# Five gradient stores cut into a 120-partition part from SyncE and an 8-partition part from ScalarE

## The chip, the core and the metric

The kernel runs on one core of a Trainium2 chip. The core has five engines that run beside each other: TensorE (PE in the profile; its weight loads are PEld), VectorE (DVE), ScalarE (ACT), GpSimd (POOL) and SyncE (SP), which here does nothing but issue transfers. Transfers between the chip's memory (HBM) and the on-chip memory of 128 partitions (SBUF) are carried out by 16 DMA engines. The metric is the time of one execution on the device, in microseconds (us).

## What is computed

The reference is the forward pass and all gradients of a decoder block for a single new token in each of B = 4 sequences: layer norm, attention with 32 heads over a cache of 4096 keys and values of size 128, output projection, then layer norm and a gated feed-forward part. What matters here are the gradients of the cache:

```python
q = ((_layernorm(x) @ wq).reshape(B, 1, H, Dh)).transpose(0, 2, 1, 3)
scores = jnp.einsum("bhqd,bhkd->bhqk", q, k_cache) * (Dh ** -0.5)
p = _softmax(scores, axis=-1)
o = jnp.einsum("bhqk,bhkd->bhqd", p, v_cache)
...
_out, _vjp = jax.vjp(_f, A_x, A_k_cache, A_v_cache, A_wq, A_wo, B_w1, B_w3, B_w2)
_grads = _vjp(grad_out)
```

For each of the B x H = 128 heads the gradient of the keys, dK = dS (outer product) q, and that of the values, dV = p (outer product) dO, are each a block of 4096 x 128 numbers in bf16, 1 MB. Reading K once and V twice and writing dK and dV moves about 640 MB.

## The kernel before, in words

A head is a tile of 128 partitions; each partition holds 32 consecutive rows of 128 numbers, which are 8 KB and contiguous in HBM on both sides. Such tiles live in 23 slots (class `Slot`): taking a slot waits until its last user is done, which for a stored tile is the landing of its store.

Two passes run over the heads. The first one loads K and V of each head, computes scores, softmax and the forward output. After a short middle part (feed-forward, its gradient, and the start of the gradient of the attention output) the second pass loads V again and works through the heads in steps of its main loop (L1252), where step s does the following:

- `load_ahead` issues the load of a later head's V on SyncE (L797).
- `front` (L1166) transposes V of head s + 5 on TensorE in groups of eight (L764), copies each group back on ScalarE (L765), and multiplies with dO (L1182). Every fourth head, ScalarE copies the result (L1157), TensorE transposes it (L1164), and `group_dS` turns it into dS for four heads on VectorE (L1196, L1199).
- `more_V` calls `grad_V` (L777), which makes the dV tile of a head some steps ahead on VectorE (the outer product of L770) and has SyncE store it (L781).
- `grad_K` (L1202) makes the dK tile of head s in the same way, and has SyncE store it (L1206).
- `step` adds a piece of the remaining work: the gradients of the weights, which are also stored by SyncE (L1101 is one of these).

The order on every engine is the order of the program, written by hand. Every transfer that SyncE or ScalarE issues gets one of eight completion semaphores in rotation; before it is issued, the transfer that last had the same semaphore must have landed. As SyncE alone issues such transfers in this kernel, it keeps eight of them in flight. At the end of the kernel SyncE waits for all that is outstanding (L1298).

At the end of the second pass V is all loaded and the weights' gradients are out; what is left in SyncE's queue is dV and dK in turn, then, as dV runs ahead, the last four dK stores in a row. The heads are called dK 0 to dK 127 and dV 0 to dV 127 in what follows.

Of the kernel before, what the change touches and what calls it, by code (L numbers as in the profile page):

```python
# [24 lines left out]
def kernel(  # L25
# [22 lines left out]
    nc = tc.nc  # L48
    P = nc.NUM_PARTITIONS
# [7 lines left out]
    NH = B * H  # L57
# [26 lines left out]
    def bh_of(s):  # L84
        return s % B, s // B

    def rows_of(ap):
        return ap.rearrange("(p j) d -> p j d", p=P)
# [89 lines left out]
    def ones_window(col):  # L178
# [11 lines left out]
                          in_=rowg[:, None, :, None].to_broadcast([P, 4, 8, 4]))  # L190
# [578 lines left out]
    def outer(dst, col2, row):  # L769
        nc.vector.tensor_tensor(  # L770
            out=dst.rearrange("p j (r t) -> p j r t", t=2),
            in0=col2[:, :, None, :].to_broadcast([P, SJ, Dh // 2, 2]),
            in1=row.rearrange("p (r t) -> p r t", t=2)[:, None, :, :].to_broadcast([P, SJ, Dh // 2, 2]),
            op=ALU.mult,
        )
# [151 lines left out]
    with ExitStack() as c2:  # L927
# [274 lines left out]
        def grad_K(s):  # L1202
            b, h = bh_of(s)
            gk = Slot("gk")
            outer(gk.heads(), dS2s[s // B][:, s % B], reps["rq", s // REP][:, s % REP, :])
            nc.sync.dma_start(out=rows_of(out_2[b, h]), in_=gk.heads())  # L1206
            gk.give()

        def prefetch():
# [42 lines left out]
        for s in range(NH):  # L1252
            load_ahead(s + L)
            if s % REP == 2:
                replicate("rq", s + 2)
            if s + L < NH:
                front(s + L)
            elif s + L == NH:
                rows_out()
                rows_T()  # L1260
            if s > 0:
                more_V(s + 1 + lead_V(s))
            grad_K(s)
            if s % B == B - 1 and s + 1 < NH:
                group_dS((s + 1) // B)
            if O0 <= s < S0:
                step("o")
            if s >= S1:
                step("s", 2)
            elif s >= O0:  # L1270
                step("q")
# [31 lines left out]
```

## Time and profile before

| | before |
|---|---|
| time, median of 3 runs | 1702.98 us (1702.85 to 1703.41) |
| span of the profiled execution | 1700.1 us |
| busy: PE, DVE, ACT, POOL | 73%, 73%, 57%, 24% |
| moved by DMA | 707.50 MB, mean 416 GB/s |
| dK stores | 128 of 1024 KB, 20.1 us from issue to landing (median) |
| dV stores | 128 of 1024 KB, 20.0 us |
| second loads of V | 128 of 1024 KB, 19.9 us |
| one dK or dV tile on VectorE | 2.29 us |
| first and last of SyncE's last ten issues | 1657.23 and 1679.34 us |

The busy shares of the engines say how long each worked, not what limits. The rows of transfers tell from issue to landing, which holds the time in the queue as well as the time of the transfer itself. The mean rate says how well the 16 DMA engines are used together. Times inside the span are counted from its start.

### The profile page before, as it was taken

The numbers are of one execution on the slowest core, as the hardware profiler recorded it, in microseconds if no ns is written. First come the engines' busy times: TensorE is split into PE (matmuls) and PEld (weight loads), VectorE is DVE, ScalarE is ACT, GpSimd is POOL, SyncE is SP. The second block draws the span as 40 slices with busy tenths as digits, with TensorE's granted clock in tenths as the row PEclk, the third lists the DMA queues.
The fourth block names the chain that finished last, engine by engine and source line by source line (L and its number), as shares of the span: only waits on it lengthen the run. The fifth ranks groups of instructions, "written<-read, shape, count | busy, mean of one in ns | idle before, by whom it ended". The sixth has DMA issues, their size and how long they took to land.

```text
span 1700.1 us, 38407 instructions
## 1 busy us (share of the span) xinstructions
PE 1242.4 (73%) x16180; PEld 915.5 (54%) x16180; DVE 1236.5 (73%) x1294; ACT 968.9 (57%) x1502; POOL 406.4 (24%) x678
## 2 busy tenths in 40 slices
PE   5889888888888888877877664786676566586550
PEld 4777676666666666655655443443444343344330
DVE  5989999999998997667776665674557466566672
ACT  3555444544454444677766564676677566576550
POOL 1211222222222231324352111142112222210120
PEclk8999999999999999799899897977799778777775
DMA  9999999999999999999999999999999999999996
GB/s 401 424 424 424 424 424 424 424 423 424 417 422 412 423 405 400 385 415 425 425 424 426 425 426 426 425 426 426 425 423 420 419 423 417 423 420 414 416 423 275
DMA packets 101741, 707.50 MB, mean 416 GB/s; under 512 B 11052, under 2 KB 15288, under 8 KB 17600
## 3 DMA queue, kind: packets, MB, share of 16 engines
q1 hardware_dynamic: 101152, 704.95, 99.4%
q8 instruction: 127, 2.08, 0.5%
q14 instruction: 46, 0.38, 0.1%
q0 software_dynamic: 416, 0.10, 0.0%
HBM read 422.59 MB, written 282.34 MB: 415 GB/s over the span
## 4 chain that ended last, share of the span: by engine, by line
DMA 37%; ACT 10%; PE 7%; issue 1%; DVE 1%; DVEq 0%; SPq 0%; ACTq 0%; POOL 0%
DMA out_dram<-gv 14%; DMA out_dram<-gk 12%; DMA V<-in_A_v_cache_dram 9%; ACT V L765 9%; PE pt_tps L764 2%; PE dq_ps L962 2%; PE dP_ps L1182 2%; DMA out_dram<-gwo 1%; DVE gk L770 1%; DVE gv L770 1%; PE rep_ps L1133 0%; ACT dPr L1157 0%; PE pt_wo L574 0%; ACT reps L1136 0%; PE o_ps L1059 0%
## 5 line engine op out<-in xcount | busy, mean ns | idle before, releaser
L765 ACT COPY V<-pt_tps 128x1024 bf16<-128x1024 bf16 x512 | 490.2, 1024 | 132.9 <-PE pt_tps L764 128.5
L764 PE MATMUL pt_tps<-ident_b,V 128*128 128x128 bf16 x4096 | 353.3, 247 | 192.4 <-ACT V L765 152.9
L764 PEld LDWEIGHTS <-V 128*128 128x128 bf16 x4096 | 303.1, 113 | 264.0 <-issue 199.0
L770 DVE TENSOR_TENSOR gv<-P,reps 128x4096 bf16<-128x4096 bf16 x125 | 286.3, 2293 | 191.3 <-DMA out_dram<-gv 100.3
L770 DVE TENSOR_TENSOR gk<-dS,reps 128x4096 bf16<-128x4096 bf16 x128 | 293.1, 2292 | 103.8 <-DMA out_dram<-gv 89.8
L421 DVE TENSOR_TENSOR PK<-Kn,PK 128x4096 bf16<-128x4096 bf16 x128 | 292.3, 2284 | 26.1 <-POOL PK L417 25.7
L436 PE MATMUL M_ps<-PK,Vn 128*128 128x130 bf16 x4096 | 284.3, 221 | 32.8 <-DMA Vn<-in_A_v_cache_dram 32.0
L436 PEld LDWEIGHTS <-Vn 128*128 128x128 bf16 x4096 | 252.0, 99 | 53.2 <-DMA Vn<-in_A_v_cache_dram 45.5
L328 DVE STREAM_TRANSPOSE KT<-Kn 128x512 f32<-128x512 f32 (+1 forms) x321 | 250.6, 797 | 0.3 <-issue 0.2
L323 ACT COPY KT<-pt_tps 128x1024 bf16<-128x1024 bf16 x128 | 129.5, 1012 | 186.4 <-PE pt_tps L322 153.0
L1182 PE MATMUL dP_ps<-V,zd 128*32 128x512 bf16 x1024 | 181.2, 431 | 68.0 <-ACT V L765 64.6
L1152 POOL COPY P<-P_all 128x64 bf16<-128x64 bf16 x125 | 100.5, 806 | 447.3 <-DVE gv L770 440.0
L1147 POOL COPY zd<-dOT_bf 128x2 bf16<-128x2 bf16 x128 | 131.4, 1028 | 155.3 <-PE dP_ps L1182 155.2
L334 POOL TENSOR_TENSOR W<-qrep,wmask 128x128 bf16<-128x128 bf16 x128 | 123.8, 967 | 82.4 <-PE S_ps L354 67.6
L417 POOL COPY PK<-P_all 128x64 bf16<-128x64 bf16 x128 | 32.6, 254 | 414.3 <-ACT P_all L411 411.3
L1182 PEld LDWEIGHTS <-zd 128*32 128x32 bf16 x1024 | 37.7, 95 | 156.5 <-issue 141.8
L411 ACT COPY P_all<-pt_P 32x64 bf16<-32x64 bf16 x256 | 52.1, 203 | 53.1 <-PE pt_P L407 50.8
L322 PE MATMUL pt_tps<-ident_b,Kn 128*128 128x128 bf16 x1024 | 80.4, 223 | 0.0
L446 PE MATMUL kP_ps<-PK,onesw 128*32 128x512 bf16 x1024 | 79.1, 386 | 0.0
L386 ACT ACTIVATE E<-S_ps,nm 128x256 f32<-128x256 f32 x64 | 30.4, 474 | 80.4 <-DVE nm L383 80.4
L322 PEld LDWEIGHTS <-Kn 128*128 128x128 bf16 x1024 | 62.0, 100 | 25.8 <-issue 25.8
L354 PE MATMUL S_ps<-KT,W 128*32 128x256 bf16 x1536 | 75.3, 285 | 0.5 <-DVE KT L328 0.2
(239 smaller groups left out, 1226.0 us busy)
## 6 DMA issues: line engine op xcount, KB each, us to landing
Kn<-in_A_k_cache_dram SPq DMA_DIRECT2D x128, 1024.0 KB, 15.4
Vn<-in_A_v_cache_dram SPq DMA_DIRECT2D x128, 1024.0 KB, 15.6
V<-in_A_v_cache_dram SPq DMA_DIRECT2D x128, 1024.0 KB, 19.9
out_dram<-gv SPq DMA_DIRECT2D x128, 1024.0 KB, 20.0
out_dram<-gk SPq DMA_DIRECT2D x128, 1024.0 KB, 20.1
wq<-in_A_wq_dram SPq DMA_DIRECT2D x8, 1024.0 KB, 15.5
out_dram<-gw SPq DMA_DIRECT2D x6, 896.0 KB, 19.8
wo<-in_A_wo_dram SPq DMA_DIRECT2D x4, 1024.0 KB, 11.7
```

The source lines that it names most:

```text
L322: nc.tensor.transpose(pt[:, i, :], Kn[:, c * GW + i, :], ident_b[:])
L323: nc.scalar.copy(out=KT[:, c * GW:(c + 1) * GW, :], in_=pt[:])
L328: nc.vector.transpose(out=KT[:, c * w_:(c + n) * w_], in_=Kn[:, c * w_:(c + n) * w_])
L334: nc.gpsimd.tensor_tensor(out=W[:, hl], in0=qrep[:, :, s:s + 1].to_broadcast([P, 4, 32]), in1=wmask[:, hl, None, :].to_broadcast([P, 4, 32 ...
L421: nc.vector.tensor_tensor(out=PK[:, :, 0:Dh].rearrange("p j (r t) -> p j r t", t=2), in0=Ks[s].heads().rearrange("p j (r t) -> p j r t", t=2),
L436: nc.tensor.matmul(hold["M"][:], lhsT=Vn[:, j, :], rhs=PK[:, j, :], start=(j == 0), stop=(j == SJ - 1))
L764: nc.tensor.transpose(pt[:, i, :], v[:, g * GW + i, :], ident_b[:])
L765: nc.scalar.copy(out=v[:, g * GW:(g + 1) * GW, :], in_=pt[:])
L770: nc.vector.tensor_tensor(out=dst.rearrange("p j (r t) -> p j r t", t=2), in0=col2[:, :, None, :].to_broadcast([P, SJ, Dh // 2, 2]), in1=r ...
L1147: nc.gpsimd.tensor_copy(out=zd[s % B][:, 32:132:67], in_=dOT_bf[:, s:s + 1].to_broadcast([P, 2]))
L1152: nc.gpsimd.tensor_copy(out=P2s[s][:], in_=P_all[:, s, :, None].to_broadcast([P, SJ, 2]))
L1182: nc.tensor.matmul(rows["acc"][32 * c:32 * (c + 1), :], lhsT=zq_window(zd[hl], 2 * hl + u), rhs=VT[:, j0:j0 + 4, :], start=(hl == 0 and u ...
```

## The change

The stores of dK for the last five heads (123 to 127) are cut in two. The first 120 partitions are issued by SyncE as before; the last 8 partitions go out as a transfer of their own, 64 KB, which ScalarE issues. It is meant to change how the rows of these last stores are spread over the DMA engines: a store of 128 rows and one of 120 and one of 8 rows need not be split in the same way.

```diff
-            nc.sync.dma_start(out=rows_of(out_2[b, h]), in_=gk.heads())
+            dk = rows_of(out_2[b, h])
+            if s < NH - 5:
+                nc.sync.dma_start(out=dk, in_=gk.heads())
+            else:
+                nc.sync.dma_start(out=dk[0:P - 8], in_=gk.heads()[0:P - 8])
+                nc.scalar.dma_start(out=dk[P - 8:P], in_=gk.heads()[P - 8:P])
             gk.give()
```

The line numbers of the changed kernel are higher by two for the whole stores (L1208); the parts stand at L1210 (SyncE) and L1211 (ScalarE).

## The prediction

> **What bounds the kernel now.** I read the slices of the page first, then the end of the run in stretches.
>
> ```profile
> DMA  9999999999999999999999999999999999999996
> GB/s 401 424 424 424 424 424 424 424 423 424 417 422 412 423 405 400 385 415 425 425 424 426 425 426 426 425 426 426 425 423 420 419 423 417 423 420 414 416 423 275
> ...
> q1 hardware_dynamic: 101152, 704.95, 99.4%
> ```
>
> The 16 DMA engines are busy throughout at about 424 GB/s; no compute engine is above 73%. Only the last slice (42.5 us) falls, to 275 GB/s. I cut it up (columns: stretch, length, busy us of PE, PEld, DVE, ACT, POOL, then clock, DMA share, GB/s):
>
> ```profile
> 1660.00:1680.00 20.00, 0.00 (x0) 0.00 (x0) 6.31 (x3) 0.00 (x0) 0.00 (x0) 0.50 1.01 426
> 1680.00:1684.00 4.00, 0.00 (x0) 0.00 (x0) 0.00 (x0) 0.00 (x0) 0.00 (x0) 0.50 0.91 385
> 1684.00:1686.00 2.00, 0.00 (x0) 0.00 (x0) 0.00 (x0) 0.00 (x0) 0.00 (x0) 0.50 0.33 139
> 1686.00:1690.00 4.00, 0.00 (x0) 0.00 (x0) 0.00 (x0) 0.00 (x0) 0.00 (x0) 0.50 0.06 27
> 1690.00:1694.00 4.00, 0.00 (x0) 0.00 (x0) 0.00 (x0) 0.00 (x0) 0.00 (x0) 0.50 0.06 27
> 1694.00:1698.00 4.00, 0.00 (x0) 0.00 (x0) 0.00 (x0) 0.00 (x0) 0.00 (x0) 0.50 0.06 27
> ```
>
> From 1686 on the DMA share is 0.06, one sixteenth: **one DMA engine works alone** while fifteen have finished, between about 1683 and 1686. The DMA view of 1686 to 1698 counts what it still moves:
>
> ```profile
> DMA packets 44, 0.32 MB, mean 27 GB/s; under 512 B 5, under 2 KB 5, under 8 KB 5
> ```
>
> 44 packets, of which 5 are semaphore writes: 39 rows of 8 KB in 12 us, so 0.306 us a row, and one transfer (128 rows over 16 engines, 8 rows each) takes an engine 8 x 0.306 + 0.006 = 2.454 us, which is the spacing of SyncE's last issues ((1679.34 - 1654.77)/10 = 2.457). Meanwhile SyncE only waits:
>
> ```profile
> SPq L1298 <- DMA out_dram<-gk: 18.9, 2, 16.6
> ```
>
> The last store is issued at 1679.34 and lands after 19.4 us (the smallest time of the gk transfers) at 1698.8; 1.3 us later the span ends. SyncE keeps 8 transfers in flight: it issues one when the one eight places earlier has landed on all engines, so the late engine sets the pace and always holds 8 x 2.454 = 19.6 us of work. The landing events of each transfer (16, one per engine) show the other fifteen done 12.6 to 15.9 us earlier, median 14.1, in each of the last fourteen. The lag grows from 1.9 us at 760 to 14 us at 1430 (time from the span's start) and then stays.
>
> [...] The trace has one late engine but no engine numbers. [...] the 8 KB transfers from GpSimd land in 5.5 us (oflat) while the late engine holds 19.6 us of SyncE's work, and in 5.4 us at the start, where it held none.
>
> **The change, part by part.** (a) *Removed*: [...] If that is the late one, it loses 5 x 2.454 = 12.3 us.
> (b) *Added*: five 64 KB transfers, one row on each of 8 engines: 5 x 0.312 = 1.6 us for each of these. The issues themselves, 0.33 us each by SyncE's rows, lie on ScalarE after its last copy:
>
> ```profile
> 1652.71 0.59 ACT L1157 COPY dPr<-dP_ps 128x512 f32<-128x512 f32 x1 [0.85 <-PE dP_ps L1182]
> ```
>
> Nothing else is queued behind them there, so they cost ScalarE nothing.
> (c) *Moved: the order of waits.* Transfers of SyncE and ScalarE share eight completion semaphores in rotation. In the changed program's waits the five small stores take five places well before SyncE reaches their heads, so SyncE skips these places, and then waits for the small stores when it comes to the same semaphores again: dK 119 waits for the small part of dK 123, dK 120 for that of 124, 121 for 125, 122 for 126, and dK 123 for that of 127. I worked this through from the landings of before (issue of the transfer eight places on):
> - dK 117 now waits one landing later: 1639.6 instead of 1637.1; dV 121 1642.1 (1639.6); dK 118 1647.1 (1642.1); dV 122 1652.2 (1644.7).
> - dK 119 waits for the small part of dK 123. VectorE writes that tile at 1649.66 to 1651.95 and ScalarE is free at 1653.3. How long does a small store take from issue to landing? No row shows it. From below: SyncE's first issue (0.74) had its first packets 1.0 to 1.5 us later; two packets (0.6 us) and the 0.37 us from the last packet to its landing at the end give 2.0 to 2.5 us. From above: GpSimd's small transfers, 5.2 to 5.9 us. I take 2.3 us, since that row has the same kind of queue. So 1655.7 instead of 1647.1.
> - dV 123 waits for dV 121's landing on the late engine: 1659.7 (1649.7).
> - dK 120 waits for the small part of dK 124. VectorE:
>
> ```profile
> 1657.42 6.69 DVE L770 TENSOR_TENSOR gk<-dS,reps 128x4096 bf16<-128x4096 bf16 x3
> ```
>
> The first of these ends at 1659.7; + 2.3 us gives 1662.1 (1652.3). Then dV 124 1662.4, dK 121 1664.3, dV 125 1664.7, dK 122 1666.5, dV 126 1667.0, dK 123 1668.8, dV 127 1669.5, and dK 124 to 127 as before, the last at 1679.3, since each of these waits for a landing on the late engine, which is never empty in all this.
>
> **The sum.** The late engine ends dV 127 at 1686.6 if it is the one left out. The fifteen others run dry between 1646 and 1661, waiting for SyncE, and this work cannot be made up. From dV 123 on they are full: first packets 1659.7 + 1.45 = 1661.1; 13 transfers x 2.454 = 31.9; four small rows 1.25 (the first one ran in the gap); landing 0.37: **1694.7**, against 1698.8. The gain is 4.1 us, not 12.3: eight of them go back to the idle fifteen. VectorE does not suffer, as the tiles it waits for come from stores before dK 119. 1703.0 - 4.1 = 1698.9; with a small allowance for a delayed row, **1699.0**.
> Bounds: a first packet after 1.0 us gives 1698.4; small stores 1 us slower put dK 120 1 us later with an empty queue ahead of it, and give 1699.5; at 5.5 us, 1701.6.
>
> **The rivals.**
> 1. *The late engine is not the one left out.* Then it carries all eight rows of every store, and its end is 1698.8, plus 1.6 us if it is among the eight that carry small rows: 1703.0 to 1704.5, slower than before by up to 0.1%. For it: no engine number in the trace[...]. [...]
> 2. *The full 12.3 us*, 1690.7: if the waits of (c) bite less than read. Against: the landing times leave no room, with SyncE's order fixed.
> 3. *Slow small stores*, as GpSimd's: 1701.0 to 1701.6, a gain under 0.2%.
> 4. *120 rows go to 8 engines, 15 rows each*: five stores each take 7 x 0.306 = 2.1 us more there, 10.7 us together, 1705.4 at the end: 1709.6, slower by 0.4%. [...]
>
> **How the numbers follow.** Main case 0.64, rival 1 0.16, rival 2 0.04, rival 3 0.11, rival 4 0.05. "Faster by over 0.2%" is below 1699.6: rival 2 and 0.85 of the main case, 0.04 + 0.54 = 0.58. Within 0.2%: the rest of the main case, rivals 1 and 3: 0.10 + 0.16 + 0.11 = 0.37. Slower: 0.05. The range takes in the main case from 1697.8 (some of the waits shorter) and rivals 3 and 1, up to 1704.6, and leaves out 2 and 4.
>
> **What would show it.** After the last issue the DMA share should stay near 0.94 (15 of 16 engines), then fall at once, with no stretch of 0.06 at 27 GB/s. Between 1642 and 1661 the share should drop well under 1, as SyncE's issues spread (gaps of 5.0, 5.1, 3.4 and 4.0 us). SyncE should have waits for a transfer of gk issued by ScalarE at dK 119 to 123, and those transfers should land in 2 to 3 us. A stretch of 0.06 that is still there makes rival 1 right; a share near 0.5 at the end, rival 4; no dip in the share before 1661 refutes (c).

## The result, and the profile after

The changed kernel takes **1710.44 us** (median of 4 runs, 1708.17 to 1712.26), the one before 1703.09: ratio 1.0042, 95% interval 1.0025 to 1.0060. Instead of 4 us won, 7 are lost. A second set of runs gave 1710.62 (5 runs, 1709.20 to 1711.79) against 1702.67: 1.0045, interval 1.0032 to 1.0057.

The forecast of 1699.0 takes it that a store of 120 rows runs on 15 engines and that the late engine is the sixteenth. No trace of the kernel before shows either; both were my assumption.

First, the page of the changed kernel: the slices, the two queues, and the rows of the cut stores.

```profile
GB/s 401 424 424 424 424 423 425 424 423 423 419 424 406 421 409 396 365 423 425 426 424 426 425 425 426 425 426 426 424 422 416 423 420 416 422 421 410 411 336 298
...
q1 hardware_dynamic: 101107, 704.62, 99.1%
...
q10 hardware_dynamic: 80, 0.33, 0.2%
...
out_dram<-gk SPq DMA_DIRECT2D x5, 960.0 KB, 24.4
...
out_dram<-gk ACTq DMA_DIRECT2D x5, 64.0 KB
```

Now two slices fall, not one: 336 and 298 GB/s. The last but one ran at 423 before. q10 is ScalarE's queue, with 40 rows of 8 KB and 40 semaphore writes: eight landings for each small store. q1 has 45 packets fewer than before (101107 against 101152), 40 rows and five semaphore writes: a store of 120 rows has 15 landings where a whole one has 16. The 120-row parts need 24.4 us from issue to landing (median); the whole dK stores need 20.1.

The end in stretches (columns as before: stretch, length, busy us of PE, PEld, DVE, ACT, POOL, then clock, DMA share, GB/s):

```profile
1640.00:1660.00 20.00, 10.94 (x88) 7.24 (x88) 13.18 (x11) 8.87 (x10) 1.34 (x1) 0.74 0.76 310
1660.00:1680.00 20.00, 0.00 (x0) 0.00 (x0) 9.35 (x5) 0.00 (x0) 0.00 (x0) 0.52 0.91 332
1680.00:1684.00 4.00, 0.00 (x0) 0.00 (x0) 0.00 (x0) 0.00 (x0) 0.00 (x0) 0.50 1.03 412
1684.00:1688.00 4.00, 0.00 (x0) 0.00 (x0) 0.00 (x0) 0.00 (x0) 0.00 (x0) 0.50 0.99 344
1688.00:1692.00 4.00, 0.00 (x0) 0.00 (x0) 0.00 (x0) 0.00 (x0) 0.00 (x0) 0.50 0.98 336
1692.00:1696.00 4.00, 0.00 (x0) 0.00 (x0) 0.00 (x0) 0.00 (x0) 0.00 (x0) 0.50 0.97 322
1696.00:1700.00 4.00, 0.00 (x0) 0.00 (x0) 0.00 (x0) 0.00 (x0) 0.00 (x0) 0.50 0.88 326
1700.00:1704.00 4.00, 0.00 (x0) 0.00 (x0) 0.00 (x0) 0.00 (x0) 0.00 (x0) 0.50 0.49 207
```

There are two different losses here, and the pair of columns "DMA share, GB/s" keeps them apart. From 1640 to 1660 the share is 0.76 at 310 GB/s: 0.76 x 424 = 322, so the engines that work do so at nearly full speed, and others are idle. From 1684 to 1696 the share is 0.97 to 0.99, but only 322 to 344 GB/s come through: the engines are *busy and slow*. Nothing like that stands in the trace before, where a share of 1.01 moved 426 GB/s.

The idle stretch comes from SyncE's waits. Its waits from 1640 on, in the changed kernel:

```profile
SPq L1208 <- DMA out_dram<-gk: 11.3, 4, 5.1
...
SPq L781 <- DMA out_dram<-gk: 4.7, 1, 4.7
```

The 5.1 us are dK 119 (issued at 1660.45) waiting for the small part of dK 123, which landed at 1660.38. The 4.7 us are dV 122, which waits for a landing on the late engine that comes later in the rotation than before. SyncE's issues stand apart by 5.0, 5.1, 5.5, 2.3 and 4.6 us from dV 121 to dK 120, where they stood 2.46 us apart before.

Two things about this profiled run. It issues the same loads of V 2.4 to 2.6 us later than before already from 1612 on (1614.46 against 1612.05), ahead of the first changed instruction; the profile of the second set of runs is not late there (0.3 us earlier than before) and has a span of 1707.3. So the change itself costs 1707.3 + 0.3 - 1700.1 = 7.5 us. And the late engine is still late. Its landings of the last transfers, read from the landing events of each store, are (us, with the distance from the one before; before, all distances are 2.4 to 2.5):

| transfer | dV 125 | dK 122 | dV 126 | dK 123 | dV 127 | dK 124 | dK 125 | dK 126 | dK 127 |
|---|---|---|---|---|---|---|---|---|---|
| late engine's landing | 1684.12 | 1686.62 | 1690.70 | 1694.15 | 1699.25 | 1701.74 | 1704.17 | 1706.65 | 1709.10 |
| distance | 2.6 | 2.5 | **4.1** | **3.5** | **5.1** | 2.5 | 2.4 | 2.5 | 2.5 |

The last landing of every cut store stands in this row, so none of them leaves the late engine out, and three transfers in the busy-and-slow stretch cost it 12.6 us instead of 7.4.

### The profile page after: what moved, and what is told of

The parts are those of the page before. It is cut to its first block, busy times and chain, and to the rows that moved or that the text cites. A ratio compares the mean times of both kernels' runs of the same rounds, so it can differ in the third digit from the quotient of the medians.

```text
span 1710.1 us, 38417 instructions
## 1 busy us (share of the span) xinstructions
PE 1239.5 (72%) x16180; PEld 915.6 (54%) x16180; DVE 1236.3 (72%) x1294; ACT 968.2 (57%) x1502; POOL 409.3 (24%) x678
## 3 DMA queue, kind: packets, MB, share of 16 engines
q1 hardware_dynamic: 101107, 704.62, 99.1%
## 4 chain that ended last, share of the span: by engine, by line
DMA 41%; ACT 6%; PE 5%; DVE 2%; issue 1%; DVEq 0%; SPq 0%; ACTq 0%; POOL 0%
DMA V<-in_A_v_cache_dram 15%; DMA out_dram<-gv 12%; DMA out_dram<-gk 11%; ACT V L765 6%; PE pt_tps L764 2%; PE dq_ps L962 1%; DMA out_dram<-gwo 1%; DMA out_dram<-gwq 1%; PE dP_ps L1182 1%; DVE gk L770 1%; DVE gv L770 1%; PE pt_wo L574 0%; PE rep_ps L1133 0%; ACT dPr L1157 0%; PE dOT_ps L737 0%
## 5 line engine op out<-in xcount | busy, mean ns | idle before, releaser
L764 PE MATMUL pt_tps<-ident_b,V 128*128 128x128 bf16 x4096 | 348.9, 245 | 195.9 <-ACT V L765 161.5
L764 PEld LDWEIGHTS <-V 128*128 128x128 bf16 x4096 | 298.5, 112 | 267.9 <-issue 211.9
L1152 POOL COPY P<-P_all 128x64 bf16<-128x64 bf16 x125 | 104.7, 839 | 440.2 <-DVE gv L770 432.9
L400 ACT ACTIVATE Pn<-E,rl 128x1024 bf16<-128x1024 f32 x64 | 73.7, 1152 | 3.2 <-DVE rl L397 3.2
## 6 DMA issues: line engine op xcount, KB each, us to landing
out_dram<-gk SPq DMA_DIRECT2D x123, 1024.0 KB, 20.1
out_dram<-gk SPq DMA_DIRECT2D x5, 960.0 KB, 24.4
```

Source lines behind the costliest of these rows:

```text
L764: nc.tensor.transpose(pt[:, i, :], v[:, g * GW + i, :], ident_b[:])
L1152: nc.gpsimd.tensor_copy(out=P2s[s][:], in_=P_all[:, s, :, None].to_broadcast([P, SJ, 2]))
```

## The experiments

**What could cost the time.** *Collision*: the late engine is not the one that a 120-row store leaves out, and stores of 120 rows slow down an engine that is still at a store of 128 rows. *Waits*: SyncE's waits for the small stores, step (c). *Small stores*: their own transfers. The first of these took its full form only after the first three kernels.

### Each part alone

`x1_main_only`: the last five dK stores are only the 120-row parts; the other 8 rows are not stored. No small stores, no changed waits. (The edits of this and the next kernel are shown against the kernel before, that of the third against the changed kernel.)

```diff
-            nc.sync.dma_start(out=rows_of(out_2[b, h]), in_=gk.heads())
+            dk = rows_of(out_2[b, h])
+            if s < NH - 5:
+                nc.sync.dma_start(out=dk, in_=gk.heads())
+            else:
+                nc.sync.dma_start(out=dk[0:P - 8], in_=gk.heads()[0:P - 8])
```

> The last five dK stores go out for 120 partitions by SyncE alone; the other 8 partitions of these five heads are not stored. So there are no small stores, and SyncE's order of waits is that of before. Theory W (the waits: SyncE waits for the small stores, and the fifteen other DMA engines run dry): all of that is gone, the late engine has 5 x 2.454 = 12.3 us less and the fifteen end at 1685 as before: 1691 us. Theory S (the shape: a store of 120 rows moves its rows more slowly than one of 128): the rate after SyncE's last issue stays near the 330 GB/s that the changed kernel shows there, instead of 15/16 of 424 = 398, and some engines end later than others: 1694 to 1702 us. Theory L (the late engine is not the one left out): no gain, 1703 us, and a stretch at 27 GB/s at the end.

`x2_small_only`: whole stores as before, and ScalarE issues five transfers of 8 partitions x 64 B from the same tiles at the same places, into a scratch tile on the chip, so that SyncE's waits are those of the changed kernel.

```diff
+        scr = bw3.tile([P, 5, 32], BF16, name="scr", tag="scr", bufs=1)
...
             nc.sync.dma_start(out=rows_of(out_2[b, h]), in_=gk.heads())
+            if s >= NH - 5:
+                nc.scalar.dma_start(out=scr[0:8, s - NH + 5, :], in_=gk.t[P - 8:P, 0:32])
```

> All dK stores go out whole by SyncE as before; ScalarE issues five extra transfers of 8 rows of 64 bytes from the same five tiles into a scratch tile, so that the rotation of semaphores and all waits are those of the changed kernel, at next to no bytes. Theory W: SyncE's issues from dK 117 to dK 123 come late as in the changed kernel, and the DMA share dips between 1642 and 1675; the late engine has 19.6 us of work in hand and may just bridge it: 1703 to 1707 us. Theory S: no 120-row store, so no loss of rate after the last issue; 1703 us, or only what the waits cost.

`x3_both_sync`: the change, with the small parts issued by SyncE behind the large ones.

```diff
-                nc.scalar.dma_start(out=dk[P - 8:P], in_=gk.heads()[P - 8:P])
+                nc.sync.dma_start(out=dk[P - 8:P], in_=gk.heads()[P - 8:P])
```

> Both parts of the last five dK stores are issued by SyncE, the small one right after the large one. The rotation then follows SyncE's own order, and nothing waits for something issued later. Theory W: the loss of the changed kernel is gone: 15 engines end at about 1685 + 5 x 0.31, the late one at 1687, so 1691 to 1693 us. Theory S: the 120-row stores are as slow as in the changed kernel, so 1695 to 1704 us. The difference to the changed kernel (1710) is what the waits cost, the difference to the first of these kernels what the small stores cost.

| kernel | time | ratio to before (95% interval) |
|---|---|---|
| x1_main_only | 1712.91 (1712.83 to 1713.85) | 1.0063 (1.0048 to 1.0078) |
| x2_small_only | 1701.95 (1701.02 to 1704.54) | 0.9996 (0.9987 to 1.0005) |
| x3_both_sync | 1712.97 (1712.34 to 1713.78) | 1.0063 (1.0048 to 1.0078) |

The 120-row parts alone do more damage than the whole change, although they move 320 KB less. The small transfers with all their waits do none. x3_both_sync, which has neither ScalarE's queue nor the crossed waits, loses as much as x1_main_only. Both kernels with 120-row parts took longer than anything that I had expected of them. Stretches of x1_main_only:

```profile
1660.00:1680.00 20.00, 0.00 (x0) 0.00 (x0) 6.58 (x3) 0.00 (x0) 0.00 (x0) 0.50 0.99 380
1680.00:1692.00 12.00, 0.00 (x0) 0.00 (x0) 0.00 (x0) 0.00 (x0) 0.00 (x0) 0.50 0.73 211
1692.00:1696.00 4.00, 0.00 (x0) 0.00 (x0) 0.00 (x0) 0.00 (x0) 0.00 (x0) 0.50 0.11 31
1696.00:1708.00 12.00, 0.00 (x0) 0.00 (x0) 0.00 (x0) 0.00 (x0) 0.00 (x0) 0.50 0.06 27
```

The last line settles step (a): one engine still works alone at 27 GB/s, for 12 us and more, and it lands each of the five 120-row stores (last landings 1697.35, 1702.26, 1704.70, 1707.16 and 1709.61). The second line is the new loss: a share of 0.73 would be 310 GB/s at full speed, and 211 came. In the landing events the late engine's distances are 3.0, 3.1, 5.6, 5.0, 4.9 and 3.9 us from 1669 to 1695, and 2.5 before and after: 25.4 instead of 14.7, **10.7 us lost**, on six stores of *128* rows. This is just while the other engines carry the five 120-row stores. The span before, 1700.1, and 10.7 make 1710.8; the span here is 1710.9.

x2_small_only:

```profile
1640.00:1660.00 20.00, 10.94 (x88) 7.24 (x88) 13.30 (x12) 8.88 (x10) 0.88 (x1) 0.74 0.67 280
1660.00:1680.00 20.00, 0.00 (x0) 0.00 (x0) 8.77 (x4) 0.00 (x0) 0.00 (x0) 0.50 0.87 362
1680.00:1696.00 16.00, 0.00 (x0) 0.00 (x0) 0.00 (x0) 0.00 (x0) 0.00 (x0) 0.50 1.01 422
1696.00:1700.00 4.00, 0.00 (x0) 0.00 (x0) 0.00 (x0) 0.00 (x0) 0.00 (x0) 0.50 0.51 211
```

The idle stretch of 1640 to 1660 is all there (0.67), SyncE's last issue is 1681.6, and no time is lost: the fifteen engines spend there the slack that they otherwise spend at the end, and finish 2.9 us ahead of the late one instead of 14. The late engine never runs dry. The waits fall as a cause, and so do the small transfers as such. These carry 64 B a row; what rows of 8 KB cost the late engine is in the sum further down.

### What slows an engine: which rows a store takes

`m1_shapes` and `m2_ports` leave out the whole computation: SyncE issues groups of 24 stores from one tile, each group with other rows; the last group of `m2_ports` has stores of 128 and 120 rows in turn. Each ran once.

```python
def stores(count, p0, p1, eng=None):
    for _ in range(count):
        d = dst()
        nc.sync.dma_start(out=d[p0:p1], in_=src_t[p0:p1, :])
```

First what was expected of `m1_shapes`, then of `m2_ports`. There, theory P says that it counts which rows a store takes, theory K that the number of engines counts, or any number of rows but 128:

> Nothing of the reference is computed: SyncE stores one tile over and over, in groups of 24 stores of 128, 120, 128, 112, 128, 96, 64, 128 rows from partition 0 on and at last 120 rows from partition 8 on, 8 KB a row. The pace of the issues is the time of one store. Theory W: 120 rows take 8 rows an engine as 128 do, 2.45 us, and have 15 landings; 112, 96 and 64 rows [...] 7/8, 6/8 and 4/8 of that: 2.14, 1.84, 1.23 us. Theory S: 120 rows take clearly longer, 3 us or more, and the other shapes show whether it is 15 engines or any shape but 128 rows that is slow.

> Nothing of the reference is computed: groups of 24 stores of one tile by SyncE, with 128 rows between the groups: rows 0 to 63, 32 to 95, 64 to 127, 0 to 104, and 128 and 120 rows in turn. Theory P: 0 to 63 and 64 to 127 take 2.45 us a store [...], 32 to 95 half of that, 1.23 us; 128 and 120 in turn take more than 2.45 us each[...]. Theory K: 32 to 95 take as long as 0 to 63; 105 rows [...] are slow in any case.

Stretches inside the groups. The busy columns are here only DVE and POOL. m1_shapes, the group of rows 0 to 119:

```profile
80.00:105.00 25.00, 0.00 (x0) 0.00 (x0) 1.00 0.95 395
```

m2_ports, in this order: 128 rows; rows 0 to 63; 32 to 95; 64 to 127; 0 to 104; 128 and 120 rows in turn:

```profile
30.00:46.00 16.00, 0.00 (x0) 0.00 (x0) 1.00 1.01 419
80.00:104.00 24.00, 0.00 (x0) 0.00 (x0) 1.00 0.99 208
185.00:208.00 23.00, 0.00 (x0) 0.00 (x0) 1.00 1.02 420
290.00:316.00 26.00, 0.00 (x0) 0.00 (x0) 1.00 0.99 207
420.00:448.00 28.00, 0.00 (x0) 0.00 (x0) 1.00 0.93 314
540.00:594.00 54.00, 0.00 (x0) 0.00 (x0) 1.00 0.94 285
```

Stores of 120 rows among themselves are harmless: 395 GB/s is 15/16 of 421, with an issue every 2.50 us (128 rows: 2.47). In turn with whole stores, a pair (248 rows of 8 KB, 2.03 MB) takes 7.1 us at 285 GB/s instead of 4.97, and a quarter of the 8 KB packets take over 550 ns, most of the others 309. Other row counts are slow even alone, against the expectation: 112 and 96 rows ran at 347 and about 315 GB/s in m1_shapes, which is 2.6 and 2.5 us a store instead of 2.14 and 1.84, and 105 rows at 314 in m2_ports (DMA share 0.93). The three groups of 64 rows show what it depends on: same bytes, same 16 engines, yet rows 32 to 95 run at 420 GB/s with 314 ns a packet, rows 0 to 63 and 64 to 127 at half of that with 627 to 629 ns. Only *which partitions* are read differs, and the rows of HBM that go with them.

What makes these rows slow and not others is not shown. Measured is that a packet takes twice as long, 627 to 629 ns against 314; the packets of over 550 ns in the mixed pair, against 309, look like the same. Whether it lies at the partitions or at the rows of HBM, no run tells, as none stores the same partitions to other rows of HBM.

### The same in the kernel

If it counts which rows a store takes, it should be seen in the kernel too: the last five dK stores can be cut to 64 rows in two ways that differ only in which 64 rows they are. Both leave the other 64 rows unstored. The edit is against the changed kernel; the first added line is x4_mid64's, the second x5_low64's.

```diff
-                nc.sync.dma_start(out=dk[0:P - 8], in_=gk.heads()[0:P - 8])
-                nc.scalar.dma_start(out=dk[P - 8:P], in_=gk.heads()[P - 8:P])
+                nc.sync.dma_start(out=dk[32:96], in_=gk.heads()[32:96])
+                nc.sync.dma_start(out=dk[0:64], in_=gk.heads()[0:64])
```

> The last five dK stores go out only for partitions 32 to 95; the other 64 rows of these heads are not stored. Theory P [...] the late engine has 5 x 4 x 0.306 = 6.1 us less: 1696 to 1698 us. Theory K (it is the number of 15 engines, or any store other than of 128 rows, that is slow): slower than 1698; no gain if any other shape disturbs.

> The twin of the run on partitions 32 to 95: the same 64 rows in number and the same 16 shares of 4, but from partitions 0 to 63; the other 64 rows of these heads are not stored. Theory P: [...] the late engine is slowed as by the 120-row stores and gains less than 6.1 us or loses: 1699 to 1710 us. Theory K: the same time as its twin.

x4_mid64 took 1696.98 (1696.00 to 1697.96), ratio 0.9969 (0.9957 to 0.9981); x5_low64 took 1706.43 (1705.63 to 1707.56), ratio 1.0024 (1.0014 to 1.0035). Stretches of x4_mid64:

```profile
1680.00:1684.00 4.00, 0.00 (x0) 0.00 (x0) 0.00 (x0) 0.00 (x0) 0.00 (x0) 0.50 0.43 180
1684.00:1692.00 8.00, 0.00 (x0) 0.00 (x0) 0.00 (x0) 0.00 (x0) 0.00 (x0) 0.50 0.06 27
```

and of x5_low64:

```profile
1680.00:1692.00 12.00, 0.00 (x0) 0.00 (x0) 0.00 (x0) 0.00 (x0) 0.00 (x0) 0.50 0.51 99
1692.00:1696.00 4.00, 0.00 (x0) 0.00 (x0) 0.00 (x0) 0.00 (x0) 0.00 (x0) 0.50 0.12 27
```

0.43 x 424 = 182: full speed. 0.51 x 424 = 216 against 99: half. Each of the five stores spares the late engine four rows, 1.23 us: 5 x 1.23 = 6.1. In x4_mid64 its landings of the stores of 128 rows are 2.4 to 2.5 us apart throughout. In x5_low64 those of the last five such stores ahead of its first cut store are 3.0, 4.3, 4.9, 4.8 and 5.1 us apart, from 1673 to 1695: 22.0 instead of 12.3, 9.8 us lost. 1702.2 - 6.1 = 1696.1 (measured 1697.0), and 1702.2 - 6.1 + 9.8 = 1705.9 (measured 1706.4). The 9.5 us between two kernels with the same bytes are the collision.

### Which engine is late

`p1_probe`: the kernel before, with nine extra SyncE transfers of 8 down to 2 rows (64 B each), spread over the second pass; one run, with a profile.

```diff
+        PROBES = {84: 8, 88: 7, 92: 6, 96: 5, 100: 4, 104: 3, 108: 2, 112: 8, 116: 7}
+        scr = bw3.tile([P, 5, 32], BF16, name="scr", tag="scr", bufs=1)
...
+            if s in PROBES:
+                n_ = PROBES[s]
+                nc.sync.dma_start(out=scr[0:n_, (s // 4) % 5, :], in_=P_all[0:n_, 0, :])
```

> The kernel before with nine tiny transfers by SyncE in the second pass, of 8, 7, 6, 5, 4, 3, 2, 8 and 7 rows of 64 bytes into a scratch tile[...]. A probe that includes the late engine has one landing some 10 to 14 us after the rest, as it stands behind that engine's queue. In the run with both parts on SyncE the 8-row stores had one such landing. [...] Time near 1703 us.

The probes of 8, 7, 6 and 5 rows each have one landing about 18 us after their issue, all others within 9.1; those of 4, 3 and 2 rows have none (all within 4.7). By these landings the late engine carries a row of each of the probes of 8 to 5 rows, and none of those of 4 to 2. The other runs agree: in x3_both_sync the eight landings of the first small part come seven early (within 4.6 us) and one at 23.3, so the late engine carries one of its rows, and in v1_one124 below it is on neither the part of 124 rows nor that of 4. With the five 120-row stores that it lands in x1_main_only, neither part of the cut leaves it out. The run took 1708.8 us, once; nothing is read from its time.

### A repetition, and a store that does leave the late engine out

`a2_after` is the changed kernel again. `v1_one124` stores one dK (head 100) as 124 + 4 rows from SyncE. No probe of 4 rows had a late landing, and I took it that both parts run on the same four engines, without the late one.

```diff
-            nc.sync.dma_start(out=rows_of(out_2[b, h]), in_=gk.heads())
+            dk = rows_of(out_2[b, h])
+            if s == 100:
+                nc.sync.dma_start(out=dk[0:P - 4], in_=gk.heads()[0:P - 4])
+                nc.sync.dma_start(out=dk[P - 4:P], in_=gk.heads()[P - 4:P])
+            else:
+                nc.sync.dma_start(out=dk, in_=gk.heads())
```

> The changed kernel again, beside the same runs of before. Theory (the late engine, which carries all eight rows of every cut store, is slowed to about half its pace while the other fifteen work on stores of 120 rows): the dK parts of 120 rows cost it up to 10 us, less where SyncE's own waits hold the fifteen back: 1708 to 1713. Rival (the time over 1708 came from a run that was late from its start, by 2.4 us, and not from the change): 1703 to 1705. If both times seen before (1708.5 and 1712.1) come back, the cut's cost itself has two values, and the difference should be in the trace after the first cut store or before it.

> One dK store (head 100) as 124 rows and 4 rows, both from SyncE. By the number of landings of the sizes seen so far [...] 124 rows go to 4 engines with 31 rows each, 4 rows to the same four; the late engine was in no probe of 4 rows, so it skips one whole transfer of 2.45 us: the lag of the late engine falls from 14.1 to 11.6 us after head 100, and the time from 1702.3 to 1699.8, if the reads of 31 rows do not collide with its own. The four engines get 32 rows, 9.8 us instead of 2.45, and have 14.1 us to spare. Rival (reads of another split collide with the late engine for as long as they last, 9.8 us at half pace): it loses 5 us and gains 2.45, 1704.8.

a2_after gave 1710.62; its stretches show the same busy-and-slow part:

```profile
1680.00:1684.00 4.00, 0.00 (x0) 0.00 (x0) 0.00 (x0) 0.00 (x0) 0.00 (x0) 0.50 0.99 350
1684.00:1688.00 4.00, 0.00 (x0) 0.00 (x0) 0.00 (x0) 0.00 (x0) 0.00 (x0) 0.50 0.99 334
1688.00:1692.00 4.00, 0.00 (x0) 0.00 (x0) 0.00 (x0) 0.00 (x0) 0.00 (x0) 0.50 0.94 332
```

The slowed landings are the same three (4.4, 3.5 and 5.1 us apart). The rival in its expectation, a run late from its start, falls.

v1_one124 gave 1703.51 (1701.78 to 1704.71), ratio 1.0004 (0.9995 to 1.0012): no change. Both parts have four landings each, as expected. The late engine does skip one transfer, and its lag falls from about 13 us to about 11 after it. But during the 124-row store, which took 17.6 us, the lag first rose to 15.5 us: two landings of the late engine stand 3.7 and 3.5 us apart, 2.3 us lost, about what it saved. SyncE's issues were up to 3.7 us apart, and afterwards four more engines were late. As the late engine had five other transfers or more in flight at each of these landings, the 2.3 us were not waiting for SyncE; they are what the rival had in mind, at about half of its size. The 1699.8 us hoped for did not come.

## Why the prediction was wrong

- **The bound** was read rightly: one late engine sets the end. x4_mid64 shows it directly: four rows fewer for it in each of five stores bring 5.3 us (6.1 by the rows).
- **Step (a) failed.** The five 120-row stores run on 15 engines (15 landings each, besides one event just after the issue), as assumed; but the late engine is one of these fifteen, and lands all five in x1_main_only. I had written that the trace has no engine numbers, and still took the late engine for the one left out, which nothing in the trace showed. The probes of p1_probe are how to ask before deciding. The term is 0 in place of -12.3 us.
- **A cost that is missing.** I took a row as 0.306 us whatever else is in flight, in the main case and in rival 1 alike. With two splits in flight at once eight rows took the late engine up to 5.6 us instead of 2.45: 10.7 us lost on six transfers in x1_main_only, 5.3 us on three in the changed kernel. Where the prediction has -12.3, a cost should have stood.
- **Step (b)** was sized rightly, 5 x 0.31 = 1.6 us (each small part takes the late engine 0.29 to 0.32 us in x3_both_sync), but for the wrong engine: it falls on the late one, as in rival 1. The time from issue to landing was taken as 2.3 us and is 4.6 and 4.5 us for the first two small stores, most of whose packets took 1.0 to 2.3 us, and 5.9 to 6.5 us for the others, beyond the upper bound of 5.9 that I had.
- **Step (c)** happened in the order worked out, with gaps of 5.0, 5.1, 5.5, 2.3 and 4.6 us against a forecast of 5.0, 5.1, 3.4, 4.0 and 2.4, as the small stores took longer, and the dip before 1661 is there. By itself it costs nothing, since without (a) the late engine is never empty: x2_small_only (ratio 0.9996).
- **The sum, corrected**: 5.3 (three slowed transfers) + 1.6 (small rows) + 0.6 left over = 7.5 us. The last two stand together in the landings: in the first profile, four of the transfers that land between 1660 and 1675, while the small rows go out, are 2.2 us longer in all. What the 0.6 is, stays open. The change loses less than x1_main_only, though it moves more: there the late engine is some 12 us, five transfers, behind the others when they start on the 120-row stores; here (c) has held them back, and it is 1.8 us behind the next and soon at 120-row stores itself. That the waits of (c) softened the collision is a reading of the two sets of landings; no run varies it alone.
- **Rivals.** Rival 1 had the right premise, and a time of 1703.0 to 1704.5 that lacks the collision. Rival 4's 1709.6 lies near the measured time by chance: it had 120 rows on 8 engines, and there are 15 landings. Of the signs named, the remaining stretch of 0.06 is plain in x1_main_only; in the changed kernel other engines, the latest only 0.2 us ahead of the last landing, cover it.

Still open: why this one engine falls behind at all, and how the other engines slow it with a 120-row store, since no run shows how the 120 rows are dealt out. No run separates the partitions read from the rows of HBM written. No version tried beats the kernel before with all its stores made.

## What to carry to other kernels

When one DMA engine ends late, find out which one before moving work off it: small transfers of 8, 7, 6... rows show by their last landing which of them it serves (in p1_probe about 18 us for 8 to 5 rows, within 4.7 us for 4 to 2). Keep all stores that are in flight together in one split over the partitions, or in one that leaves their pace as it is, as rows 32 to 95 did (the late engine's landings of whole stores stayed 2.4 to 2.5 us apart); another, such as 120 rows, can be cheap alone (395 GB/s) and still halve the pace of its neighbours (up to 5.6 us for a whole store's eight rows instead of 2.45). And read the DMA share beside the GB/s: here a low share at its full rate (0.76 at 310 GB/s) was waiting, and a full share at a low rate (0.97 at 322) was a collision.

## What the hardware showed that was not expected

- Rows 0 to 63 are stored at 208 GB/s, rows 32 to 95 of the same tile at 420.
- Stores of 128 and of 120 rows in turn run at 285 GB/s, though either alone runs at 419 and 395.
- Leaving the small part out makes the kernel no faster: 120 rows instead of 128 are issued every 2.50 us instead of 2.47 among themselves, as each of 15 engines has eight rows.
